# Converting the early weight tiles first and letting attention normalise later, in a fused attention and two-layer kernel

## The chip, the cores and the metric

The kernel runs on one core of one Trainium2 chip. The metric is the time of one execution in device microseconds; the time quoted for a kernel is the median of its runs. A profile is one execution with the hardware profiler on; its span is measured from the first to the last instruction shown.

## The reference

Batch 2, 8 heads, 768 positions, head size 64. Attention with a local window of 96 positions and 8 global ones, then two dense layers, all in float32:

```python
scores = q @ k.T / 8 - slope[h] * dist;  outside the window: -1e9
a = softmax(scores);  x = (a @ v) as 1536 tokens x 512
h = x @ w_in;   x = (h * tanh(softplus(h))) @ w_out      # layer 1, d_ff 2048
h = x @ w_in2;  out = softplus(h) @ w_out2               # layer 2
```

## The kernel before

**Attention** works in 24 steps. A step is one batch, one pair of heads and two query tiles of 128 rows, so four score tiles, each against at most 232 keys. `scores` (L462) puts them into PSUM, `soft` adds the bias and takes the row extreme on VectorE (L481) and the exponential with its row sum on ScalarE (L492). `norm` adds 1e-9 to the four sums on GpSimd (L501), takes the reciprocal on VectorE (L503) and multiplies the four tiles on GpSimd (L506). `transposes` turns the tiles on TensorE (L522) and copies them to SBUF on ScalarE or VectorE (L525), `values` multiplies by v (L539), and `store_x` writes x as a rounded half and a rest (L553 ScalarE, L554 VectorE). In one turn of the loop the program writes down the scores of step i, `norm` of step i-1, `transposes` of i-2, `values` of i-3 and `store_x` of i-4. The tiles of probabilities have LAG+2 = 4 buffers, the small tiles m and z three each (pool `sb`). The loads of q, k, v and the raw weights all go through one DMA queue, that of SP.

**The dense layers** see 3 blocks of 512 tokens. Each layer has 16 weight tiles f; tile f has two halves, part 0 for the up product (w_in) and part 1 for the down product (w_out). A chunk s is one layer, one block and one f. `up(s)` is 12 matmuls (L247) into one PSUM bank; `chunk(s)` is the activation and the split of its result into a rounded half and a rest (for layer 1: four VectorE instructions L104, L106, L109, L115, four ScalarE ones L102, L107, L110, L282, one GpSimd L283); `down(s)` is 12 matmuls (L267) into four banks `yp`. Program order puts `down(s-3)` behind `up(s)`.

**Weights** arrive as float64 bit patterns and are made into float32 pairs by the core itself, in 64 units of one half tile. A unit is three VectorE instructions (L145, L150, L154, 128x512 each), a ScalarE copy (L209) and a GpSimd subtraction (L211); `fill(upto)` advances this by ticks, four to a unit. The units of layer 1 are in the order (0,0) (1,0) (2,0) (3,0) (0,1) (4,0) (1,1) (5,0) (2,1) (6,0) (3,1) (7,0) (4,1) (8,0) (5,1) ..., written as (tile, part). Tiles 0 to 6 (EARLY = 7) have SBUF of their own; tiles 7 to 14 use the pool `wb`, which is opened only when attention has given its SBUF back.

**Beside each other.** `norm` carries `fill` with a goal that rises to 4*PRE = 40 ticks, so 10 units, by the end of attention; `early` writes the first AHEAD = 4 chunks into the attention loop, at turns 15, 17, 19 and 21. From chunk 4 on the goal rises by RATE1 = 8 ticks, so two units, with each chunk. This is program order. The framework makes the queue of each engine from it: an instruction with a higher place in program order is preferred, one that is ready earlier by its own model of the durations may go ahead of it, except that the first instruction of each unit keeps its place among its kind. Once the queues are made, each engine runs its queue in order.

Of the kernel before, what the change touches and what calls it, by code (L numbers as in the profile page):

```python
# [11 lines left out]
F32 = mybir.dt.float32  # L12
# [8 lines left out]
P = 128  # L21
# [4 lines left out]
NK = G + W + P  # L26
# [4 lines left out]
FC = DFF // P  # L31
TB = 512
# [3 lines left out]
WMIN2 = float((np.array([0x38100000], np.int32).view(np.float32) ** 2)[0])  # L36
CUTS = ((0, P + NK, 0, 2 * P), (P + NK, P + 3 * NK, 2 * P, 4 * P), (P + 3 * NK, KX, 4 * P, S))
SKEW = 3
PRE = 10
EARLY = 7  # L40
DLAG = 3
LAG = 2
AHEAD = 4
FROM = 15
HPO = 60
RATE1 = 8.0
RATE2 = 4.5
WEIGH = ((14, 1.2, 24), (65, 1.45, 40))

# [109 lines left out]
def fast_path(tc, small, qT, kx, vx, w1, w2, out, ng, nl, two, load_flag):  # L159
    nc = tc.nc  # L160
    far_side = bass.opposite_side(tc.default_side)
    with ExitStack() as outer:
# [8 lines left out]
        raw = {}  # L171

        units = []
        for n in range(0, 2 * FC, FC):
            for f in range(FC + SKEW):
                units += [(n + f, 0)] if f < FC else []
                units += [(n + f - SKEW, 1)] if f >= SKEW else []

        turns = []
        for i in range(2):  # L180
# [41 lines left out]
        def xy_tile(name):  # L222
            return xy.tile([P, CC, 2, TB], F32R, tag="xy", name=name)

        x = [xy_tile(f"x{i}") for i in range(NB)]
# [4 lines left out]
        gp = outer.enter_context(tc.tile_pool(name="gp", bufs=2))  # L230
# [4 lines left out]
        g = {}  # L235
# [103 lines left out]
        def early(i):  # L339
            s, odd = divmod(i - FROM, 2)  # L340
            if 0 <= s < AHEAD and not odd:
                up(s)
                chunk(s, 0)

        attention(tc, qT, kx, vx, ng, nl, x, fetch, fill, early)

        wpool.append(outer.enter_context(tc.tile_pool(name="wb", bufs=FC - EARLY - 1)))
        op = outer.enter_context(tc.tile_pool(name="op", bufs=1))
# [4 lines left out]
        for s in range(DLAG, NS + DLAG):  # L353
# [6 lines left out]
            if AHEAD <= s < NS:  # L360
                up(s)
                r = s - (NB - 1) * FC
                goal = 4 * PRE + int(RATE1 * (s + 1 - AHEAD))
                if goal > 8 * FC:
# [9 lines left out]
        return general  # L374


def attention(tc, qT, kx, vx, ng, nl, x, fetch, fill, early):
    nc = tc.nc
    with ExitStack() as st:
        cst = st.enter_context(tc.tile_pool(name="cst", bufs=1))  # L380
        kv = st.enter_context(tc.tile_pool(name="kv", bufs=2))
        sb = st.enter_context(tc.tile_pool(name="sb", bufs=3))
        pts = st.enter_context(tc.tile_pool(name="pts", bufs=4))
        ps = st.enter_context(tc.tile_pool(name="ps", bufs=LAG + 2))
        pss = st.enter_context(tc.tile_pool(name="pss", bufs=1, space=PSUM))
# [7 lines left out]
        def load_qk(bh):  # L393
            if bh >= B * HP:
                return
            b, hp = bh // HP, bh % HP
            ktile[bh] = kv.tile([P, KX], F32, tag="k", name=f"k{bh}")
            qtile[bh] = kv.tile([P, S], F32, tag="q", name=f"q{bh}")
            cuts = CUTS if bh == 0 else ((0, KX, 0, S),)
            for k0, k1, q0, q1 in cuts:  # L400
                nc.sync.dma_start(ktile[bh][:, k0:k1], kx[b, hp, :, k0:k1])
                nc.sync.dma_start(qtile[bh][:, q0:q1], qT[b, hp, :, q0:q1])

        def load_v(bh):
            if bh >= B * HP:
                return
            vtile[bh] = kv.tile([P, NV, P], F32, tag="v", name=f"v{bh}")
            nc.sync.dma_start(vtile[bh], vx[bh // HP, bh % HP])
# [5 lines left out]
        load_qk(1)  # L414
        load_v(1)

        ci = cst.tile([P, P], F32, name="ci")
        rel = cst.tile([P, NK + P], F32, name="rel")
        nc.gpsimd.iota(rel[:, :NK], [[-1, NK]], base=G + W, channel_multiplier=1, allow_small_or_imprecise_dtypes=True)
        nc.gpsimd.iota(rel[:, NK:], [[-1, P]], base=0, channel_multiplier=1, allow_small_or_imprecise_dtypes=True)  # L420
        nc.gpsimd.iota(ci, [[1, P]], base=0, channel_multiplier=0, allow_small_or_imprecise_dtypes=True)
        far = cst.tile([P, NK + P], F32, name="far")
        dist = cst.tile([P, NK + P], F32, name="dist")
        nc.vector.tensor_scalar(out=dist, in0=rel, scalar1=0.0, scalar2=1000.0, op0=ALU.is_lt, op1=ALU.mult)
        nc.vector.tensor_tensor(out=rel, in0=rel, in1=dist, op=ALU.add)
        nc.vector.memset(far[:, G:NK], BIG)
# [8 lines left out]
        def slope(h):  # L435
            engine = nc.vector if h < 2 else nc.gpsimd
            engine.tensor_scalar(
                out=d8[:, h, :], in0=dist, scalar1=-8.0 * 2.0 ** -(h + 1), scalar2=1.0, op0=ALU.mult, op1=ALU.mult
            )
# [6 lines left out]
        n = len(steps)  # L446
# [3 lines left out]
        def geom(t):  # L450
            return (P, P, 1) if t == 0 else (NK, CH, 2)

        def scores(i):
            b, hp, t0 = steps[i]
            bh = b * HP + hp
            for u in range(2):
                t = t0 + u
                w, _, _ = geom(t)
                off = 0 if t == 0 else P + (t - 1) * NK
                for j in range(2):  # L460
                    rows = slice(64 * j, 64 * j + 64)
                    nc.tensor.matmul(  # L462
                        sp[:, j, u, :w],
                        qtile[bh][rows, t * P : (t + 1) * P],
                        ktile[bh][rows, off : off + w],
                        start=True,
                        stop=True,
                    )

        def soft(i):  # L470
            b, hp, t0 = steps[i]
            p = ps.tile([P, 4, NK], F32, tag="p", name=f"p{i}")
            m = sb.tile([P, 4], F32, tag="m", name=f"m{i}")
            z = sb.tile([P, 4], F32, tag="z", name=f"z{i}")
            exps = []
            for u in range(2):
                w, _, _ = geom(t0 + u)
                off = NK if t0 + u == 0 else 0
                for j in range(2):
                    c = 2 * u + j  # L480
                    nc.vector.tensor_tensor_reduce(  # L481
                        out=p[:, c, :w],
                        in0=sp[:, j, u, :w],
                        in1=d8[:, 2 * hp + j, off : off + w],
                        scale=-0.125,
                        scalar=3.0e38,
                        op0=ALU.add,
                        op1=ALU.min,
                        accum_out=m[:, c : c + 1],
                    )  # L490
                    exps.append(
                        lambda c=c, w=w: nc.scalar.activation(  # L492
                            p[:, c, :w], p[:, c, :w], AF.Exp, bias=m[:, c : c + 1], scale=-1.0, accum_out=z[:, c : c + 1]
                        )
                    )
            prob[i], psums[i] = p, z
            return exps

        def norm(i, goal):
            p, z = prob[i], psums.pop(i)  # L500
            nc.gpsimd.tensor_scalar(out=z, in0=z, scalar1=1e-9, scalar2=1.0, op0=ALU.add, op1=ALU.mult)  # L501
            fill(goal)
            nc.vector.reciprocal(z, z)  # L503
            for c in range(4):
                w, _, _ = geom(steps[i][2] + c // 2)
                nc.gpsimd.tensor_scalar(  # L506
                    out=p[:, c, :w],
                    in0=p[:, c, :w],
                    scalar1=z[:, c : c + 1],
                    scalar2=1.0,  # L510
                    op0=ALU.mult,
                    op1=ALU.mult,
                )

        def transposes(i):
            p = prob.pop(i)
            for u in range(2):
                _, ch, nch = geom(steps[i][2] + u)
                tp = pst.tile([P, 4, P], F32, tag="t", name=f"t{i}_{u}")
                for j in range(2):  # L520
                    for c in range(nch):
                        nc.tensor.transpose(tp[:ch, j * nch + c, :], p[:, 2 * u + j, c * ch : (c + 1) * ch], ident)  # L522
                t = pts.tile([P, 4, P], F32, tag="pt", name=f"pt{i}_{u}")
                copy = nc.vector.tensor_copy if (2 * i + u) % 3 == 2 else nc.scalar.copy
                copy(t[:ch, : 2 * nch, :], tp[:ch, : 2 * nch, :])  # L525
                pt[i, u] = t
# [28 lines left out]

        for i in range(n + LAG + 3):
            exps = []
            if i < n:
                scores(i)
                exps = soft(i)  # L560
                if i % per == per - 1:
                    load_qk(i // per + 2)
                if i + 2 < H:
                    slope(i + 2)
            if 0 <= i - 1 < n:
                norm(i - 1, 4 * PRE * max(0, i - 2) // (n - 2))
            for e in exps[:2]:
                e()
            if 0 <= i - LAG < n:
                transposes(i - LAG)  # L570
            for e in exps[2:]:
                e()
            if 0 <= i - LAG - 1 < n:
                values(i - LAG - 1)
                if (i - LAG - 1) % per == per - 1:
                    load_v((i - LAG - 1) // per + 2)
            if 0 <= i - LAG - 2 < n:
                store_x(i - LAG - 2)
            early(i)
# [182 lines left out]
```

## Time and profile before

| | |
|---|---|
| median of 3 runs | 649.25 us (648.32, 649.25 and one of 1016.29) |
| profiled execution: time, span | 647.7 us, 645.9 us |
| TensorE matmul busy | 614.1 us, 95% |
| TensorE weight load busy | 488.3 us, 76% |
| VectorE busy | 481.5 us, 75% |
| ScalarE busy | 344.0 us, 53% |
| GpSimd busy | 267.0 us, 41% |

Busy time is the time in which the engine had an instruction running; on TensorE matmuls overlap, so its busy share says that it had work, not that it went at its full rate. PE is TensorE, PEld its weight loads, DVE VectorE, ACT ScalarE, POOL GpSimd, SP the queue that issues the DMAs. A number after L is a line of the kernel.

### The profile page before, as it was taken

Reading aid. Unit: us, or ns where it says so; the run is one execution under the profiler, and the core shown is the slowest. Engines: PE = TensorE matmul, PEld = TensorE weight load, DVE = VectorE, ACT = ScalarE, POOL = GpSimd, SP = SyncE. Lnnn points to the kernel's source line nnn. Section 1 sums busy time; section 2 is a strip of 40 time slices with the busy share of each in tenths; the row PEclk is TensorE's granted clock in tenths of the full one; section 3 lists DMA queues with packets and bytes.
Section 4 is the critical chain, followed back from the end, with each engine's and each line's share of the span. In section 5 each row is a group of like instructions: output and inputs, shape, how many; then the busy total and the mean of one; then the engine's idle time right before and its main releaser. Section 6 shows DMA issues by size and latency. Waiting matters only on the chain. (4 is left out here: it accounts for less than half of the span.)

```text
span 645.9 us, 9028 instructions
## 1 busy us (share of the span) xinstructions
PE 614.1 (95%) x3026; PEld 488.3 (76%) x3026; DVE 481.5 (75%) x998; ACT 344.0 (53%) x715; POOL 267.0 (41%) x297
## 2 busy tenths in 40 slices
PE   5999897969999999999999999999999999999994
PEld 3666675856678888888888888888888888888883
DVE  4788888089999775656897998988778865756642
ACT  4779886155545544444555665555554444444441
POOL 5566666146654232222553554654523222132221
PEclk9999799979999999999999999999999999999998
DMA  8747513035555353431342432432445544644301
GB/s 287 231 166 280 199 48 112 21 97 157 163 170 164 129 162 100 130 98 65 90 135 70 128 101 70 142 114 71 128 142 180 165 131 131 227 132 130 131 1 71
DMA packets 24390, 85.11 MB, mean 132 GB/s; under 512 B 2832, under 2 KB 3600, under 8 KB 24336
## 3 DMA queue, kind: packets, MB, share of 16 engines
q1 hardware_dynamic: 24336, 84.46, 40.7%
q8 instruction: 26, 0.43, 0.3%
q14 instruction: 28, 0.23, 0.1%
HBM read 81.30 MB, written 3.15 MB: 131 GB/s over the span
## 5 line engine op out<-in xcount | busy, mean ns | idle before, releaser
L283 POOL TENSOR_TENSOR g<-e,g 128x512 fp32r<-128x512 f32 x96 | 131.0, 1365 | 256.2 <-ACT g L282 250.5
L247 PE MATMUL h<-x,w 128*128 128x512 f32 x576 | 146.6, 399 | 3.5 <-POOL w L211 2.2
L267 PE MATMUL yp<-g,w 128*128 128x512 f32 x576 | 142.5, 397 | 6.5 <-ACT w L209 5.5
L267 PE MATMUL yp<-w,g 128*128 128x512 f32 x576 | 139.6, 390 | 1.3 <-POOLq L97 0.7
L247 PE MATMUL h<-y,w 128*128 128x512 f32 x576 | 139.2, 390 | 0.0
L267 PEld LDWEIGHTS yp<-g,w 128*128 128x128 f32 x576 | 108.8, 191 | 33.1 <-ACT w L209 6.7
L247 PEld LDWEIGHTS h<-x,w 128*128 128x128 f32 x576 | 108.2, 191 | 30.8 <-POOL w L211 4.6
L267 PEld LDWEIGHTS yp<-w,g 128*128 128x128 f32 x576 | 107.8, 188 | 25.1 <-POOLq L97 1.1
L247 PEld LDWEIGHTS h<-y,w 128*128 128x128 f32 x576 | 108.1, 188 | 22.8
L211 POOL TENSOR_TENSOR w<-a,w 128x512 fp32r<-128x512 f32 x64 | 84.6, 1322 | 74.4 <-ACT w L209 73.7
L282 ACT CAST g<-e 128x512 fp32r<-128x512 f32 x96 | 59.4, 618 | 48.6 <-PE yp L267 44.4
L209 ACT CAST w<-a 128x512 fp32r<-128x512 f32 x64 | 39.6, 619 | 42.5 <-DVE a L154 42.1
L127 DVE SCALAR_TENSOR_TENSOR h<-h,t 128x512 f32<-128x512 f32 x48 | 33.5, 697 | 35.5 <-ACT t L125 35.4
L107 ACT ACTIVATE t<-e,two 128x512 f32<-128x512 f32 x48 | 34.7, 725 | 43.2 <-DVE e L106 43.2
L119 ACT ACTIVATE e<-h 128x512 f32<-128x512 f32 x48 | 28.5, 594 | 43.8 <-PE h L247 33.6
L102 ACT ACTIVATE e<-h 128x512 f32<-128x512 f32 x48 | 28.4, 596 | 41.9 <-PE h L247 28.9
L492 ACT ACTIVATE p<-p,m 128x232 f32<-128x232 f32 (+1 forms) x96 | 44.5, 466 | 11.3 <-DVE m L481 11.1
L115 DVE TENSOR_TENSOR e<-h,t 128x512 f32<-128x512 f32 x48 | 33.0, 687 | 23.0 <-ACT t L110 22.4
L506 POOL TENSOR_SCALAR p<-p,z 128x232 f32<-128x232 f32 (+1 forms) x96 | 42.5, 461 | 15.8 <-DVE z L503 14.6
L125 ACT ACTIVATE t<-t 128x512 f32<-128x512 f32 x48 | 30.3, 631 | 34.9 <-DVE e L124 34.8
L315 DVE CUSTOM_DVE_ANT_0 top<-top 128x512 f32<-128x512 f32 x64 | 47.9, 767 | 0.0
L145 DVE TENSOR_SCALAR bits<-raw 128x512 int32<-128x512 int32 x64 | 44.0, 688 | 4.7 <-DMA raw<-w 4.3
(64 smaller groups left out, 633.8 us busy)
## 6 DMA issues: line engine op xcount, KB each, us to landing
raw<-w SPq DMA_DIRECT2D x64, 512.0 KB, 3.5
top<-w SPq DMA_DIRECT2D x64, 512.0 KB, 3.6
v<-vx SPq DMA_DIRECT2D x8, 704.0 KB, 5.9
k<-kx SPq DMA_DIRECT2D x7, 644.0 KB, 3.8
out<-o SPq DMA_DIRECT2D x12, 256.0 KB, 3.6
q<-qT SPq DMA_DIRECT2D x7, 384.0 KB, 4.4
k<-kx SPq DMA_DIRECT2D x2, 232.0 KB, 3.6
q<-qT SPq DMA_DIRECT2D x3, 128.0 KB, 3.7
```

Of the source, the lines that this page charges most:

```text
L107: nc.scalar.activation(t, e, AF.Ln, bias=two)
L127: nc.vector.scalar_tensor_tensor(out=h, in0=h, scalar=0.0, in1=t, op0=ALU.max, op1=ALU.add)
L145: nc.vector.tensor_scalar(out=t, in0=top, scalar1=3, scalar2=0x3FFFFFF8, op0=ALU.logical_shift_left, op1=ALU.bitwise_and)
L209: nc.scalar.copy(w[:, 0, half], a)
L211: nc.gpsimd.tensor_tensor(out=w[:, 1, half], in0=a, in1=w[:, 0, half].bitcast(F32), op=ALU.subtract)
L247: nc.tensor.matmul(h, w[:, a, c * P : (c + 1) * P], src[:, c, b, :], start=(n == 0), stop=(n == 3 * CC - 1))
L267: ins = nc.tensor.matmul(yp[s // FC][c], lhsT, rhs, start=(f == 0 and a + b == 0), stop=(f == FC - 1 and b == 1))
L282: nc.scalar.copy(gg[:, 0, :], e)
L283: nc.gpsimd.tensor_tensor(out=gg[:, 1, :], in0=e, in1=gg[:, 0, :].bitcast(F32), op=ALU.subtract)
L315: nc.vector.tensor_tensor_reduce(out=top, in0=top, in1=top, scale=-1.0, scalar=-3.0e38, op0=ALU.mult, op1=ALU.max, accum_out=lows[:, u : u ...
L492: lambda c=c, w=w: nc.scalar.activation(p[:, c, :w], p[:, c, :w], AF.Exp, bias=m[:, c : c + 1], scale=-1.0, accum_out=z[:, c : c + 1])
L506: nc.gpsimd.tensor_scalar(out=p[:, c, :w], in0=p[:, c, :w], scalar1=z[:, c : c + 1], scalar2=1.0, op0=ALU.mult, op1=ALU.mult,)
```

## The change

The units of tiles 0 to 6 come first, both parts, then those of tiles 7 to 15. The first 11 units are the same as before; then come (4,1) (5,1) (6,1) and only then (7,0) (8,0) (9,0) (10,0) (7,1) .... Attention's fill goal rises to 4*14 ticks over one turn more, and the goal after it by 7 ticks with each chunk. `norm` works two steps behind the scores, `transposes` three, `values` four, `store_x` five; the loop has one turn more, the tiles of probabilities have one buffer more, and the early chunks stand at turns 16, 18, 20 and 22. Four constant tiles of attention's set-up move into the two buffers of the pool `gp`, which the chunks' results use later.

```diff
-PRE = 10
+PRE = 14
 EARLY = 7
 DLAG = 3
-LAG = 2
+LAG = 3
 AHEAD = 4
-FROM = 15
+FROM = 16
 HPO = 60
-RATE1 = 8.0
+RATE1 = 7.0
...
-        for n in range(0, 2 * FC, FC):
-            for f in range(FC + SKEW):
-                units += [(n + f, 0)] if f < FC else []
-                units += [(n + f - SKEW, 1)] if f >= SKEW else []
+        for first, last in ((0, EARLY), (EARLY, FC), (FC, 2 * FC)):
+            for n in range(first, last + SKEW):
+                units += [(n, 0)] if n < last else []
+                units += [(n - SKEW, 1)] if n - SKEW >= first else []
...
-        attention(tc, qT, kx, vx, ng, nl, x, fetch, fill, early)
+        attention(tc, qT, kx, vx, ng, nl, x, fetch, fill, early, gp)
...
-        ci = cst.tile([P, P], F32, name="ci")
-        rel = cst.tile([P, NK + P], F32, name="rel")
+        spare = [gp.tile([P, 2 * TB], F32, tag="g", name=f"spare{i}") for i in range(2)]
+        rel, far, ci = spare[0][:, : NK + P], spare[0][:, TB : TB + NK + P], spare[1][:, TB : TB + P]
+        dist = spare[1][:, : NK + P]
...
-        far = cst.tile([P, NK + P], F32, name="far")
-        dist = cst.tile([P, NK + P], F32, name="dist")
...
-            if 0 <= i - 1 < n:
-                norm(i - 1, 4 * PRE * max(0, i - 2) // (n - 2))
+            if 0 <= i - 2 < n:
+                norm(i - 2, 4 * PRE * max(0, i - 2) // (n - 1))
```

## Rows read from the trace of the kernel before

**Rows 1.** Stretches: busy us (instructions) by engine, granted clock, DMA share, GB/s.

```profile
20.00:40.00 20.00, 18.42 (x153) 11.98 (x150) 15.78 (x69) 15.70 (x56) 11.90 (x27) 1.00 0.65 207
40.00:60.00 20.00, 20.00 (x187) 14.26 (x185) 16.40 (x64) 16.69 (x62) 14.91 (x32) 1.00 0.63 229
60.00:80.00 20.00, 16.98 (x111) 12.11 (x110) 16.64 (x58) 17.21 (x55) 12.32 (x22) 0.83 0.61 208
80.00:95.00 15.00, 15.00 (x122) 11.36 (x121) 11.88 (x42) 11.46 (x34) 10.68 (x21) 1.00 0.14 42
95.00:112.00 17.00, 14.04 (x128) 10.15 (x125) 15.39 (x43) 12.43 (x38) 11.00 (x19) 1.00 0.36 118
112.00:131.00 19.00, 18.38 (x91) 14.40 (x90) 4.29 (x9) 4.18 (x9) 2.58 (x2) 1.00 0.10 29
...
141.00:185.60 44.60, 41.49 (x169) 30.42 (x168) 41.31 (x68) 24.32 (x41) 26.82 (x21) 1.00 0.51 157
...
200.00:500.00 300.00, 299.92 (x1320) 247.43 (x1320) 238.73 (x394) 158.10 (x268) 120.39 (x89) 1.00 0.37 116
```

**Rows 2.** TensorE in order of time: start, us, what [idle before <-releaser].

```profile
112.92 4.90 PE L267 MATMUL yp<-g,w 128*128 128x512 f32 x20 [0.51 <-ACT x L553]
117.75 1.09 PE L539 MATMUL xhalf<-pt,v 116*64 116x128 f32 x16
118.78 6.45 PE L267 MATMUL yp<-g,w 128*128 128x512 f32 x27
125.06 2.88 PE L247 MATMUL h<-x,w 128*128 128x512 f32 x12
...
128.01 2.88 PE L247 MATMUL h<-x,w 128*128 128x512 f32 x12
135.99 5.16 PE L267 MATMUL yp<-g,w 128*128 128x512 f32 x12 [5.10 <-ACT w L209]
140.98 2.92 PE L247 MATMUL h<-x,w 128*128 128x512 f32 x12
```

**Rows 3.** The stretch of that wait in slices of 5 us, columns as in rows 1.

```profile
135.00:140.00 5.00, 4.01 (x10) 3.10 (x11) 4.93 (x9) 2.70 (x5) 2.10 (x2) 0.50 0.41 123
```

**Rows 4.** VectorE in order of time, columns as in rows 2.

```profile
110.45 0.69 DVE L154 SCALAR_TENSOR_TENSOR a<-raw,bits 128x512 int32<-128x512 int32 x1
...
128.61 0.92 DVE L104 TENSOR_SCALAR t<-e 128x512 f32<-128x512 f32 x2 [7.72 <-ACT e L102]
...
132.67 0.68 DVE L145 TENSOR_SCALAR bits<-raw 128x512 int32<-128x512 int32 x1
```

**Rows 5.** VectorE until 112.8 us, by line: count, busy us, mean ns, idle before.

```profile
L145 DVE TENSOR_SCALAR bits<-raw 128x512 int32<-128x512 int32 x12 | 8.3, 691 | 0.4 <-DMA raw<-w 0.4
L150 DVE SCALAR_TENSOR_TENSOR bits<-raw,bits 128x512 int32<-128x512 int32 x12 | 8.3, 690 | 0.1
L154 DVE SCALAR_TENSOR_TENSOR a<-raw,bits 128x512 int32<-128x512 int32 x12 | 8.2, 683 | 0.2
...
L503 DVE RECIPROCAL z<-z 128x4 f32<-128x4 f32 x24 | 4.1, 173 | 12.0 <-POOL z L501 11.6
...
L106 DVE SCALAR_TENSOR_TENSOR e<-e,t 128x512 f32<-128x512 f32 x5 | 3.5, 696 | 0.1
L109 DVE TENSOR_TENSOR h<-e,h 128x512 f32<-128x512 f32 x5 | 3.4, 688 | 0.1
L115 DVE TENSOR_TENSOR e<-h,t 128x512 f32<-128x512 f32 x5 | 3.4, 684 | 0.1
L104 DVE TENSOR_SCALAR t<-e 128x512 f32<-128x512 f32 x5 | 2.2, 447 | 0.5 <-ACT e L102 0.4
```

**Rows 6.** GpSimd and ScalarE late in attention, in order of time.

```profile
98.36 1.58 POOL L506 TENSOR_SCALAR p<-p,z 128x128 f32<-128x128 f32 x4 [0.38 <-DVE z L503]
99.90 1.27 POOL L211 TENSOR_TENSOR w<-a,w 128x512 fp32r<-128x512 f32 x1
...
101.98 0.49 ACT L492 ACTIVATE p<-p,m 128x232 f32<-128x232 f32 x1 [0.35 <-DVE m L481]
```

More of the change, by code (lines that the diff above doesn't have):

```diff
@@ L374, in fast_path, with attention @@
         return general
-def attention(tc, qT, kx, vx, ng, nl, x, fetch, fill, early):
+def attention(tc, qT, kx, vx, ng, nl, x, fetch, fill, early, gp):
     nc = tc.nc
```

## Prediction

> **What bounds the kernel now.** I read the stretches first [rows 1]. From 200 to 500 us TensorE is never idle: 1320 matmuls in 300 us, 227.3 ns each, all of 512 columns. The change touches nothing there, so this is the pace against which the rest is measured. The loss lies ahead of it, in three places.
>
> The first is attention. Between 20 and 112 us VectorE is busy for 15.78 + 16.40 + 16.64 + 11.88 + 15.39 = 76.1 of 92 us and TensorE for 84.4 of 92 [rows 1]. Neither is full throughout; from 60 to 80 us the mean granted clock is 0.83.
>
> The second is the hand-over. The order of TensorE's work [rows 2] shows 48 matmuls of down 0 to 3 (20, 27, and one that lies between the two ups of 12 each behind them), the two ups, and then 5.10 us of nothing, ended by the ScalarE copy of a weight half (L209). It is (4,1), the thirteenth unit: down(4) needs it. The twelve matmuls that follow take 5.16 us until the next group begins about 5.0 us later, and the granted clock of that slice is 0.50, so 1.2 of 2.4 GHz [rows 3]. From 112.92 to 140.98 TensorE did 48 + 24 + 12 = 84 matmuls, worth 84 x 0.2273 = 19.1 us, and 1.09 us of attention: 28.06 - 20.2 = **7.9 us lost**.
>
> Why was (4,1) late? VectorE ended the last instruction of the twelfth unit, (7,0), at 111.1, and began (4,1) at 132.67 [rows 4]. In between it stood 7.72 us before L104, for the exponential of a chunk whose up came at 125.06 behind the downs [rows 2, 4]; in the stretch from 112 to 131 us it worked 4.29 of 19 us [rows 1]. The unit had no missing input that the trace names; it stood behind the chunk in VectorE's queue.
>
> The third is the stretch from 141 to 185.6 us. TensorE does 168 matmuls (169 by the window's count, one at its edge), worth 38.2 us, in 44.6: **6.4 us lost**. VectorE is busy 41.31 of 44.6 [rows 1], so it is the bound. Per chunk it has 0.447 + 0.696 + 0.688 + 0.684 = 2.52 us, and two units of 0.691 + 0.690 + 0.683 = 2.06 us [rows 5], 6.64 us together, where TensorE needs 24 x 0.2273 = 5.46. The measured period is 44.6 / 7 = 6.37 us (VectorE's instructions overlap slightly).
>
> **The change part by part.**
>
> *The order of units.* The first eleven are as before. Twelfth to fourteenth become (4,1), (5,1), (6,1), whose SBUF is there from the start, in place of (7,0), (4,1), (8,0). By 112.8 us the kernel before had already converted 12 units on VectorE, two more than its goal of 10 [rows 5]. With the new goal of 14, the halves for down(4), down(5) and down(6) are there when attention ends, and the wait of rows 2 has no cause: behind the two ups TensorE has down(4) to down(6), 36 x 0.2273 = 8.2 us of work, as cover for (7,0) and those behind it. With the wait goes the half-rate group. Gain between 0 (another late thing takes its place, say the result of chunk 5, which needs VectorE as well) and 7.9 us. I take 7, nearest to the full end, since the two late things in the rows are this half tile and the clock that followed.
>
> *RATE1 from 8 to 7.* Units per chunk fall from 2 to 1.75, VectorE's demand from 6.64 to 2.52 + 3.61 = 6.13 us, still over 5.46. Scaled from the measured period that is 6.37 x 6.13 / 6.64 = 5.88, a gain of 0.49 us for each of seven chunks, **3.4 us**. Bounds: 0 if VectorE again begins late and has the same backlog, 6.4 if it begins at 112 us and TensorE never sees it. The units left after attention are 18 against 20 not yet converted there in the kernel before.
>
> *More units inside attention.* Between 12 (what is there now) and 14 lie 2 x 2.06 = 4.1 us of VectorE; if the queue again runs two ahead of its goal, 16, 8.2 us. Each also has 1.27 us on GpSimd [rows 6] and a ScalarE copy. VectorE has 15.9 us free between 20 and 112 [rows 1], so some of it is hidden; where VectorE is full, it is not.
>
> *The deeper lag.* Nothing is added but a turn of the loop: the same instructions, each further from its producer. What it can remove is waiting on the chain from exponential to transpose: VectorE stood 11.6 us before its 24 reciprocals for GpSimd's sums [rows 5]. That is the cover for the extra units. I count 4.1 us of units less a part of these waits, 2.6 us, **+1.5 us** for attention as a whole. Bounds: +8.2 (four units on the path, no wait saved) and -6.4 (about two thirds of the 11.6 us returned beyond the units' cost, in turns where VectorE is what ends last). One edge gets tighter: z has three buffers still, and the exponential of step i can write only when GpSimd's multiplies of step i-3 are done. They now stand one turn later.
>
> *SP's queue.* The raw loads of the extra units (512 KB each) go into the one DMA queue ahead of later q, k and v loads. Its share in attention is 0.65 at most over 20 us and 0.14 to 0.36 in the later part [rows 1]; I cost them at nothing. If that cover is gone, a late k or v stops a step, as any late load would.
>
> *FROM and the constants in `gp`.* Four constant tiles take the two buffers that chunks 2 and 3 use later; the last reader is GpSimd's bias of head 7 in turn 5. Nothing, unless a chunk wanted them before.
>
> **Sum.** -7.0 - 3.4 + 1.5 = -8.9 us on a span of 645.9, which goes to 637.0; the profiled execution's 647.7 to 638.8. The median of the runs is 1.55 us above that execution, so the forecast is 649.25 - 8.9 = **640 us**.
>
> **The rivals.**
>
> *Attention tightens as well.* With more slack TensorE waits for less, and VectorE starts on units in the hand-over. The whole loss of 7.9 + 6.4 goes and attention shrinks by about 4 us: 649.25 - 18.3 = 631. For it: 11.6 us of reciprocal waits, and 14.7 us of idle VectorE in the hand-over [rows 1, 5]. Against: from 95 to 112 us VectorE is already busy 15.39 of 17 [rows 1]. In weight loads TensorE is far from full in attention: 59.9 of 92 us, 65%, where the dense stretch has 247.4 of 300, 82% [rows 1]; at the dense share the same loads would fit in 59.9 / 0.825 = 72.6 us, so up to 19 us are there. The Trainium skill (Perfetto Trace Analysis, Identifying the Most-Contended Engine) says to judge TensorE's headroom by weight-load occupancy and not by matmul busy time. By that rule attention has the room that this rival needs; by busy time (84.4 of 92) it has 7.6 us. The trace does not decide, since attention's matmuls are of other shapes.
>
> *The gap moves.* PE's downs again stand ahead of the up that feeds VectorE, chunk 5's result is late instead of a weight half, and attention pays for its units: -3.4 + 4.1, so 650 us. For it: the 7.72 us before L104 come from the order of TensorE's queue, which the diff does not fix [rows 2, 4]. That the order of units does not do what it says is this case too.
>
> *Slower: the sums' buffers.* GpSimd's multiplies of step 21 ended at 99.94 and the exponential of step 23 began at 101.98, 2.0 us later [rows 6]; with the new lag those multiplies stand where step 20's are needed by step 23, so this is the margin. If a unit's GpSimd subtraction of 1.27 us and a late sum use it up, ScalarE stands before the exponential, and the copies behind it in its queue with it. A subtraction each for 14 units is 17.8 us on the chain; with the units' 8.2 us and 7.9 us of the hand-over won, 649.25 + 18.1 = 667. It decides from the point where those multiplies end more than 2.0 us later than now relative to the scores. GpSimd is busy 60.8 of 92 us in attention [rows 1], which speaks against it in most steps.
>
> **How the numbers follow.** Forecast (634 to 646) 0.53, attention tightens (625 to 634) 0.21, the gap moves (646 to 656) 0.19, slower (656 to 675) 0.07. Two per cent, about what a measurement of this kernel can tell from no change, is 13 us: faster means below 636.3, slower above 662.2. Faster is the second case, 0.21, and the lower end of the first, 0.05: 0.26. Slower is most of the last, 0.05. The rest is 0.69. The range that leaves out about 0.1 on each side runs from 630 to 653.
>
> **What would show it.** After attention no TensorE wait of over 2 us on a copy of L209; down(4) to down(6) run without one; the clock stays at full rate around it. By the last instruction of attention at least 14 runs of L154, in place of 12. Attention's last matmul between 110 and 120 us in place of 118.8. A period of about 5.9 us per chunk in the VectorE-bound stretch. The reciprocal's wait well under 11.6 us. Wrong would be: attention longer by over 8 us, ScalarE waiting before L492 for GpSimd's L506, or a new idle stretch of TensorE in front of an up that waits for (7,0) or (8,0).

## The result and the profile after

| | before | after |
|---|---|---|
| median | 649.07 us (4 runs) | 641.63 us (4 runs) |
| profiled execution: time, span | 647.7, 645.9 us | 642.0, 640.1 us |

The changed kernel takes 0.9887 of the time of before (95% interval 0.9868 to 0.9906): a gain of 1.1%, less than the 2% that the prediction took as its limit, but clear of no change. The forecast was 640 us in a range of 630 to 653. One early run of the kernel before took 1016 us; it is left out of the ratio, and without it the median before is 648.89 us, so the medians differ by 7.3 us.

The stretches of the changed kernel, columns as in rows 1:

```profile
20.00:40.00 20.00, 18.25 (x152) 11.95 (x151) 17.23 (x69) 16.32 (x56) 13.34 (x29) 1.00 0.69 217
40.00:60.00 20.00, 18.45 (x166) 12.94 (x163) 18.05 (x70) 16.70 (x61) 15.95 (x34) 1.00 0.73 259
60.00:80.00 20.00, 18.94 (x157) 13.65 (x157) 19.21 (x69) 19.29 (x66) 14.03 (x26) 1.00 0.59 208
80.00:95.00 15.00, 14.73 (x114) 11.27 (x113) 14.76 (x44) 13.42 (x38) 13.42 (x24) 1.00 0.35 108
95.00:112.00 17.00, 12.49 (x99) 9.26 (x98) 12.21 (x31) 9.54 (x29) 8.50 (x14) 0.80 0.31 103
112.00:131.00 19.00, 19.00 (x105) 15.13 (x106) 4.01 (x8) 2.78 (x6) 3.84 (x3) 1.00 0.20 58
...
141.00:185.60 44.60, 41.44 (x174) 31.55 (x174) 42.20 (x68) 25.17 (x42) 24.94 (x20) 1.00 0.50 149
...
200.00:500.00 300.00, 299.81 (x1320) 247.38 (x1319) 237.89 (x394) 158.16 (x268) 120.02 (x88) 1.00 0.37 115
```

Against [rows 1] VectorE is busier in attention (17.23 + 18.05 + 19.21 + 14.76 + 12.21 = 81.5 of 92 us, where it was 76.1), the dense stretch is the same, and between 112 and 131 us VectorE is as idle as before: 4.01 of 19 us, against 4.29.

TensorE behind attention, columns as in rows 2:

```profile
111.88 5.36 PE L267 MATMUL yp<-g,w 128*128 128x512 f32 x22 [0.88 <-DVE pt L524]
117.17 1.09 PE L538 MATMUL xhalf<-pt,v 116*64 116x128 f32 x16
118.19 5.50 PE L267 MATMUL yp<-g,w 128*128 128x512 f32 x23
123.62 1.09 PE L538 MATMUL xhalf<-pt,v 116*64 116x128 f32 x16
124.64 3.69 PE L267 MATMUL yp<-g,w 128*128 128x512 f32 x15
128.17 5.60 PE L247 MATMUL h<-x,w 128*128 128x512 f32 x24
136.36 3.04 PE L247 MATMUL h<-x,w 128*128 128x512 f32 x12 [2.59 <-DVE e L115]
139.24 4.92 PE L267 MATMUL yp<-g,w 128*128 128x512 f32 x21
...
161.67 2.56 PE L247 MATMUL h<-x,w 128*128 128x512 f32 x10 [0.35 <-POOL w L211]
...
168.06 2.60 PE L247 MATMUL h<-x,w 128*128 128x512 f32 x10 [0.61 <-POOL w L211]
...
174.48 2.56 PE L247 MATMUL h<-x,w 128*128 128x512 f32 x10 [0.63 <-POOL w L211]
```

The 5.10 us wait for a weight half and the half-rate group behind it [rows 2, 3] are gone: down 0 to 4, 60 matmuls, run before the first late up, and none waits on L209. What is left there is 2.59 us before an up that has no free bank of PSUM (the memory TensorE writes its products to) until VectorE has ended a chunk (L115). From 161.67 to 174.48 the ups follow each other every 6.4 us, and each waits for GpSimd's half of a weight (L211).

VectorE there, in order of time:

```profile
114.29 0.69 DVE L154 SCALAR_TENSOR_TENSOR a<-raw,bits 128x512 int32<-128x512 int32 x1
118.71 0.42 DVE L553 TENSOR_TENSOR x<-xhalf,x 128x256 fp32r<-128x256 f32 x1 [3.74 <-ACT x L552]
125.17 0.42 DVE L553 TENSOR_TENSOR x<-xhalf,x 128x256 fp32r<-128x256 f32 x1 [6.03 <-ACT x L552]
126.57 0.42 DVE L553 TENSOR_TENSOR x<-xhalf,x 128x256 fp32r<-128x256 f32 x1 [0.98 <-ACT x L552]
132.18 0.92 DVE L104 TENSOR_SCALAR t<-e 128x512 f32<-128x512 f32 x2 [5.18 <-ACT e L102]
```

It stands from 115.0 to 132.2 us but for three short stores: for the last steps' x, whose `values` lie between the downs in TensorE's queue, and then for the exponential of a chunk whose up came at 128.17. VectorE until 112.8 us, by line, as in rows 5:

```profile
L154 DVE SCALAR_TENSOR_TENSOR a<-raw,bits 128x512 int32<-128x512 int32 x15 | 10.2, 680 | 0.2
...
L502 DVE RECIPROCAL z<-z 128x4 f32<-128x4 f32 x24 | 4.2, 173 | 8.2 <-POOL z L500 7.8
```

15 units are through, where there were 12 (a sixteenth ends at 115.0), and the reciprocals' wait fell from 11.6 to 7.8 us [rows 5].

### The profile page after: what moved, and what is told of

It is laid out like the page before. It is cut to its first block, busy times and chain, and to the rows that moved or that the text cites. A ratio compares the mean times of both kernels' runs of the same rounds, so it can differ in the third digit from the quotient of the medians.

```text
span 640.1 us, 9030 instructions
## 1 busy us (share of the span) xinstructions
PE 609.8 (95%) x3026; PEld 487.4 (76%) x3026; DVE 481.3 (75%) x998; ACT 343.8 (54%) x715; POOL 267.1 (42%) x297
## 5 line engine op out<-in xcount | busy, mean ns | idle before, releaser
L247 PE MATMUL h<-x,w 128*128 128x512 f32 x576 | 142.9, 394 | 6.0 <-DVE e L115 2.9
L267 PE MATMUL yp<-w,g 128*128 128x512 f32 x576 | 139.6, 390 | 1.5 <-POOLq L97 0.7
L267 PE MATMUL yp<-g,w 128*128 128x512 f32 x576 | 139.2, 391 | 1.7 <-DVE pt L524 0.9
L247 PEld LDWEIGHTS h<-x,w 128*128 128x128 f32 x576 | 106.6, 188 | 32.1 <-POOL w L211 4.1
L267 PEld LDWEIGHTS yp<-g,w 128*128 128x128 f32 x576 | 107.6, 188 | 26.1 <-POOL w L211 1.3
L267 PEld LDWEIGHTS yp<-w,g 128*128 128x128 f32 x576 | 107.8, 188 | 25.2 <-POOLq L97 1.1
L211 POOL TENSOR_TENSOR w<-a,w 128x512 fp32r<-128x512 f32 x64 | 84.9, 1328 | 68.8 <-ACT w L209 67.4
L282 ACT CAST g<-e 128x512 fp32r<-128x512 f32 x96 | 59.4, 620 | 47.3 <-PE yp L267 41.5
L209 ACT CAST w<-a 128x512 fp32r<-128x512 f32 x64 | 39.6, 620 | 38.5 <-DVE a L154 38.3
L119 ACT ACTIVATE e<-h 128x512 f32<-128x512 f32 x48 | 28.6, 596 | 43.8 <-PE h L247 33.6
L115 DVE TENSOR_TENSOR e<-h,t 128x512 f32<-128x512 f32 x48 | 33.0, 687 | 22.9 <-ACT t L110 22.4
L102 ACT ACTIVATE e<-h 128x512 f32<-128x512 f32 x48 | 28.5, 597 | 38.8 <-PE h L247 26.6
```

What stands on the lines that cost most here:

```text
L209: nc.scalar.copy(w[:, 0, half], a)
L211: nc.gpsimd.tensor_tensor(out=w[:, 1, half], in0=a, in1=w[:, 0, half].bitcast(F32), op=ALU.subtract)
L247: nc.tensor.matmul(h, w[:, a, c * P : (c + 1) * P], src[:, c, b, :], start=(n == 0), stop=(n == 3 * CC - 1))
L267: ins = nc.tensor.matmul(yp[s // FC][c], lhsT, rhs, start=(f == 0 and a + b == 0), stop=(f == FC - 1 and b == 1))
L282: nc.scalar.copy(gg[:, 0, :], e)
```

## The experiments

To compare kernels whose TensorE queues differ, each span is divided into three parts. **A**, attention: the start of the first down, plus 1.09 us for each step of `values` that comes later, less 0.2273 us for each matmul of an up that came earlier. The dense work: 96 chunks of 24 matmuls, 2304 in all, at the pace of [rows 1], 523.7 us, the same for all. **L**, what is left: the time lost from the hand-over on. Some 10 us of L, before and after, lie behind the stretches that are looked at here, at the block changes and the end of the kernel. Before: A = 112.92 + 1.09 - 72 x 0.2273 = 97.6, L = 645.9 - 97.6 - 523.7 = 24.6. These are of one profiled execution each. Three kernels have the same instructions in the same order on every engine (the change, the run with 8 ticks and the one with four buffers for the sums); they differ by up to 1.0 us in A and 1.6 in L, so less than that means nothing.

| kernel | first down | ups before | values later | span | A | L | median us | ratio (95%) |
|---|---|---|---|---|---|---|---|---|
| before | 112.92 | 72 | 1 | 645.9 | 97.6 | 24.6 | 649.07 | 1 |
| the change | 111.88 | 72 | 2 | 640.1 | 97.7 | 18.7 | 641.63 | 0.9887 (0.9868 to 0.9906) |
| order and goal, old lags | 115.32 | 72 | 0 | 637.2 | 99.0 | 14.5 | 639.82 | 0.9876 (0.9860 to 0.9893) |
| lags alone | 108.95 | 72 | 2 | 644.7 | 94.8 | 26.2 | 646.62 | 0.9977 (0.9965 to 0.9989) |
| change, 8 ticks | 110.87 | 72 | 2 | 638.6 | 96.7 | 18.2 | 641.61 | 0.9907 (0.9881 to 0.9933) |
| change, other bank | 110.10 | 84 | 2 | 632.6 | 93.2 | 15.7 | 635.03 | 0.9802 (0.9780 to 0.9824) |
| order and goal, bank | 121.71 | 84 | 0 | 640.4 | 102.6 | 14.1 | 640.50 | 0.9869 (0.9852 to 0.9885) |
| bank alone | 113.30 | 84 | 1 | 638.9 | 95.3 | 19.9 | 640.42 | 0.9865 (0.9848 to 0.9881) |
| change, four sums | 111.19 | 72 | 2 | 640.5 | 97.0 | 19.8 | 641.51 | 0.9883 (0.9862 to 0.9903) |
| change, goal 10 | 111.87 | 72 | 2 | 658.1 | 97.7 | 36.7 | 658.58 | 1.0138 (1.0116 to 1.0160) |
| lags and bank | 111.58 | 84 | 2 | 640.9 | 94.7 | 22.5 | 643.45 | 0.9919 (0.9903 to 0.9936) |
| change, bank, goal 12 | 113.36 | 84 | 2 | 635.3 | 96.5 | 15.1 | 637.56 | 0.9840 (0.9814 to 0.9866) |
| change, bank, goal 13 | 113.09 | 84 | 2 | 638.0 | 96.2 | 18.1 | 640.69 | 0.9880 (0.9863 to 0.9897) |
| order alone, goal 10 | 113.49 | 72 | 1 | 655.5 | 98.2 | 33.6 | 657.47 | 1.0131 (1.0104 to 1.0157) |

**Order and goal without the lags.**

```diff
-LAG = 3
+LAG = 2
-FROM = 16
+FROM = 15
-            if 0 <= i - 2 < n:
-                norm(i - 2, 4 * PRE * max(0, i - 2) // (n - 1))
+            if 0 <= i - 1 < n:
+                norm(i - 1, 4 * PRE * max(0, i - 2) // (n - 2))
```

> The changed kernel with the lags of before (normalise one step behind, transpose two, early chunks at turns 15 to 21, goal in attention over 22 turns); the order of units, the goal of 14 units and the constants' place are those of the change. Theory A (the gain is the hand-over's: the halves for down 4 to 6 are ready): 641 to 645 us, no TensorE wait on the copy of L209 behind the first ups. Rival B (the gain needs the lag, since the extra units hold up attention without it): 647 to 652 us, attention's last transposes 4 us or more later.

Measured 639.82 us, ratio 0.9876, 1.2 us below the range of theory A. Its interval and that of the change overlap over most of their length: the lags add nothing that can be seen to the order with the goal. A is 1.3 us over before, hardly more than the noise, L 10.1 under. The hand-over of this kernel, TensorE in order of time:

```profile
115.32 8.35 PE L267 MATMUL yp<-g,w 128*128 128x512 f32 x29
123.50 2.88 PE L247 MATMUL h<-x,w 128*128 128x512 f32 x12
126.22 4.47 PE L267 MATMUL yp<-g,w 128*128 128x512 f32 x19
130.53 2.88 PE L247 MATMUL h<-x,w 128*128 128x512 f32 x12
```

There is no wait at all in it, as theory A had said, though VectorE stands 9.09 us before L104 in this kernel too, until 127.05 us: 16 units were through, and TensorE had work. Rival B is out.

**The lags alone.** The units' loop, the goal of 10 and the 8 ticks are put back:

```diff
-PRE = 14
+PRE = 10
-RATE1 = 7.0
+RATE1 = 8.0
-        for first, last in ((0, EARLY), (EARLY, FC), (FC, 2 * FC)):
...
+        for n in range(0, 2 * FC, FC):
...
```

> The changed kernel with the old order of units, the goal of 10 units in attention and 8 ticks per chunk; only the lags, the turns of the early chunks and the constants' place are changed. Theory A: the wait of down(4) for its weight half is there as before, 647 to 651 us. Rival B (the lag is what gained): 641 to 644 us, with attention's end 3 us or more earlier than in the kernel before.

646.62 us, 0.9977, between the two forecasts and 0.4 us from theory A's. A falls by 2.8 us, so the deeper lag does shorten attention. But the old wait is there, and longer:

```profile
133.81 5.49 PE L267 MATMUL yp<-g,w 128*128 128x512 f32 x12 [5.75 <-ACT w L209]
```

L is 1.6 us higher, no more than kernels with the same queues differ by; the span is 1.2 us shorter. VectorE stands behind attention here as well: its last unit, the twelfth, begins its last instruction at 109.70 us, and the next L104 comes at 126.46.

**Eight ticks per chunk.**

```diff
-RATE1 = 7.0
+RATE1 = 8.0
```

> The changed kernel with 8 ticks per chunk in place of 7. Theory A of the prediction (the goal sets VectorE's load, 6.13 against 6.64 us per chunk): 644 to 646 us. Rival C (a chunk uses up two units whatever the goal says, one for its up and one for its down, and VectorE's queue has them in the same order): within 1 us of the changed kernel, 641 to 643 us, with the same period of 6.4 us per chunk.

641.61 us against 641.63. Rival C holds; theory A's term is nothing. The ups of this kernel:

```profile
160.71 2.56 PE L247 MATMUL h<-x,w 128*128 128x512 f32 x10 [0.35 <-POOL w L211]
...
167.10 2.60 PE L247 MATMUL h<-x,w 128*128 128x512 f32 x10 [0.61 <-POOL w L211]
...
173.53 2.58 PE L247 MATMUL h<-x,w 128*128 128x512 f32 x10 [0.60 <-POOL w L211]
```

The period is 6.4 us with 7 ticks, with 8 ticks and in the kernel before [rows 1], and in the traces every engine has the same instructions in the same order for 7 and 8: the edit changes nothing that runs, and this run is a repeat of the change. The goal is not what sets the rate. With 7 ticks it is 56 + 7 x 7 = 105 ticks at chunk 10, 26 units; VectorE began the last instruction of its eleventh chunk (L115) at 157.03 us with 21 units through (L154). It is behind the goal, and a lower goal takes nothing from it. A chunk needs one half for its up and one for its down; when there is no stock of halves, it costs two units: from that L115 to the one at 182.14 us there are four chunks and eight units.

**Another bank for chunk 5.**

```diff
-        h = hps[s >= AHEAD and s % 3 == 2].tile([P, TB], F32, tag="h", name=f"h{s}")
+        h = hps[s > AHEAD and s % 3 == 1].tile([P, TB], F32, tag="h", name=f"h{s}")
```

Of three banks for h the third is free only when attention's last x is stored. In both kernels of the case up(5) is the first that needs it; here it is up(7).

> The changed kernel with another choice of the PSUM bank for h: chunks 5 and 6 use the two banks that are there during attention, and the bank freed by attention's last step serves chunks 7, 10, 13 and so on. Theory D (VectorE is idle in the hand-over because up(5) has to wait for attention's last bank, and the 2.59 us wait of TensorE comes from that): 636 to 640 us, that wait gone and VectorE's idle stretch after 114 us shorter by 4 us or more. Rival E (VectorE stands in front of the last stores of x anyway, so the bank changes nothing): 641 to 643 us.

635.03 us, ratio 0.9802: the fastest of all, clear of the change by its interval, and 1 us below theory D's range. Rival E is out. TensorE in it:

```profile
97.94 3.03 PE L247 MATMUL h<-x,w 128*128 128x512 f32 x12
...
126.39 0.62 PE L247 MATMUL h<-x,w 128*128 128x512 f32 x2
126.84 1.98 PE L267 MATMUL yp<-g,w 128*128 128x512 f32 x8
128.65 5.15 PE L247 MATMUL h<-x,w 128*128 128x512 f32 x22
...
163.13 0.73 PE L247 MATMUL h<-x,w 128*128 128x512 f32 x2 [0.86 <-ACT w L209]
```

and the end of VectorE's stand:

```profile
122.55 0.43 DVE L104 TENSOR_SCALAR t<-e 128x512 f32<-128x512 f32 x1 [5.20 <-ACT e L102]
```

One up more (84 matmuls, not 72) runs inside attention, at 97.94, where the changed kernel was about to stand: its TensorE waited 2.23 and 1.00 us between 98 and 103 us, and its granted clock in the two slices of 5 us from 100 to 110 us was 0.65 and 0.67. With the other bank it is 1.00 in both. The changed kernel's slices, columns as in rows 1:

```profile
100.00:105.00 5.00, 3.18 (x24) 2.62 (x25) 2.42 (x6) 2.70 (x10) 3.23 (x7) 0.65 0.36 102
105.00:110.00 5.00, 4.61 (x32) 3.38 (x30) 3.89 (x7) 1.94 (x5) 0.19 (x1) 0.67 0.02 7
```

VectorE goes on at 122.55 instead of 132.18, and TensorE has no wait of any size until 163. A is 4.5 us lower than in the change, L 3.0.

The 5.20 us that are left are not this bank's. The exponential that VectorE waits for (L102, at 121.92) is of a chunk whose up ran at 97.94. ScalarE stood before it at the copy of an earlier chunk's result (L282, at 119.90), 3.01 us for a down (L267), and then 1.39 us for GpSimd. The results have two buffers from chunk 2 on (pool `gp`), and chunk 4's can be written when down(2) is done. More buffers there were not tried.

**The bank alone, in the kernel before, and with the old lags.** The same line as above, in the kernel before and in the first experiment's.

> The kernel before with only the other choice of the PSUM bank for h. Theory D (the chunk that VectorE waited for kept (4,1) behind it): with chunk 5 early, (4,1) is converted before down(4) needs it even in the old order, 640 to 645 us. Rival A (the order of units alone decides): the wait on L209 stays and it is 647 to 650 us.

> The new order of units and goal of 14 with the lags of before, and the other choice of the PSUM bank for h (chunks 5 and 6 on the banks that are there during attention). Theory D (the late up(5) keeps VectorE idle whatever the lag): 633 to 637 us, VectorE's wait of 9.1 us before L104 behind attention's end gone or halved. Rival F (without the lag TensorE has no gap after attention, so nothing is left to gain): 639 to 641 us.

Alone it takes the kernel before to 640.42 us, 0.9865, as theory D had it: one line does as much as the whole change, with the order of units and the goal of before. VectorE has converted (4,1) and one unit more by 120.4 us, ahead of the chunk that it waits for until 125.72:

```profile
119.76 0.68 DVE L154 SCALAR_TENSOR_TENSOR a<-raw,bits 128x512 int32<-128x512 int32 x1
...
125.72 0.43 DVE L104 TENSOR_SCALAR t<-e 128x512 f32<-128x512 f32 x1 [4.95 <-ACT e L102]
```

and down(4), the twelve matmuls at 128.31, has no wait and does not run at half rate:

```profile
117.44 8.31 PE L267 MATMUL yp<-g,w 128*128 128x512 f32 x35
125.59 2.88 PE L247 MATMUL h<-x,w 128*128 128x512 f32 x12
128.31 2.88 PE L267 MATMUL yp<-g,w 128*128 128x512 f32 x12
```

With order and goal but the old lags it gives 640.50, 0.9869, nothing beyond the order: rival F's figure, and theory D's time missed, though VectorE's wait of 9.1 us is gone as it had said. A and L show why: L is 14.1 (TensorE never waits from 121.71 to 193 us), no less than the 14.5 without the bank's line within the noise, as rival F had it, and A is 102.6: an up of 12 matmuls stands at 101.89, and among the transposes and values behind it TensorE waits 1.44 us for GpSimd and 2.37 us for a store of x. Why the framework's order came out so was not followed further.

**Lags and bank.**

> The old order of units with goal 10 and 8 ticks per chunk, the lags of the change, and the other choice of the PSUM bank for h: the last of the eight combinations of order, lag and bank. Theory D+ (the lag shortens attention by about 3 us and the bank takes the hand-over's gap, so both count): 636 to 639 us. Rival H (either the order or the bank takes the gap, and the lag is lost behind it, as in the run with the lag alone): 640 to 642 us.

643.45 us, 0.9919, worse than either rival's figure and than the bank alone; A is 94.7, but L is 22.5. A wait for a weight half is back: 2.22 us on L209 at 141.90, and the twelve matmuls behind it take 4.88 us. So of the eight combinations of order with goal, lags and bank, all three together are the best (0.9802); every other change lies between 0.9865 and 0.9977. The lags are worth 0.7% behind both others, 0.2% alone, nothing behind the order, and cost 0.5% behind the bank.

**Four buffers for the sums.**

```diff
-        sb = st.enter_context(tc.tile_pool(name="sb", bufs=3))
+        sb = st.enter_context(tc.tile_pool(name="sb", bufs=4))
```

> The changed kernel with four buffers in place of three for the small tiles of extremes and sums; the queues of all engines have the same order. The slower rival of the prediction (the exponential waits for GpSimd's multiplies three steps back): 640 us or less, by 0.5 us or more for each step where it happened. Theory A (that edge is never the last): 641 to 643 us, no difference.

641.51 us, no difference. In the changed kernel ScalarE's exponentials wait for VectorE's extremes alone. The slower rival of the prediction did not occur.

**A goal of 10, with and without the lags.** The change with the old goal, and the new order alone, which has the lags, FROM and `norm`'s line of before as well:

```diff
-PRE = 14
+PRE = 10
-RATE1 = 7.0
+RATE1 = 8.0
```

> The changed kernel with the goal in attention back at 10 units and 8 ticks per chunk; order and lags are those of the change. Theory A (it is the order that makes (4,1) to (6,1) ready, and the higher goal that puts them into attention): the halves come late again, a wait of TensorE on L209 or L211 of 2 us or more behind attention, 644 to 649 us. Rival G (VectorE's free time at the end of attention does them in any case): 640 to 643 us, with attention's end up to 3 us earlier.

> The new order of units and the constants' place, everything else as in the kernel before (lags, goal of 10 units, 8 ticks per chunk): the order by itself. Theory K (VectorE takes about 12 units by the end of attention whatever their order, stands still behind it, and the place of the thirteenth unit then decides; the order pays only with the goal of 14): 650 to 660 us, with TensorE waits of over 4 us on the copy of L209. Theory A as the prediction put it (the order makes the halves of down 4 to 6 ready by itself): 640 to 646 us.

658.58 and 657.47 us, ratios 1.0138 and 1.0131: **the order by itself makes the kernel slower**, by 1.4% with the lags and 1.3% without. The first is beyond both of its forecasts (theory A's sign, a late half, came true, its size not); the second is as theory K had it. TensorE in the second one:

```profile
136.54 8.32 PE L267 MATMUL yp<-g,w 128*128 128x512 f32 x24 [5.12 <-ACT w L209]
144.70 5.60 PE L247 MATMUL h<-x,w 128*128 128x512 f32 x24
156.46 1.22 PE L247 MATMUL h<-x,w 128*128 128x512 f32 x2 [6.16 <-ACT w L209]
158.51 7.15 PE L247 MATMUL h<-x,w 128*128 128x512 f32 x22 [0.83 <-POOL w L211]
```

Both kernels had 12 units through VectorE when attention ended, as the kernel before and the one with the lags alone had. The thirteenth, (5,1), came behind the idle stretch, so down(5) waited, 5.12 us; and now the halves for the ups are the last in the row, so an up waits too, 6.16 us. With the lags these waits are 8.02 and 6.17 us. In the old order no wait of over 0.6 us follows the one of 5.10 until 200 us. Between the waits the clock was low for a part: 24 matmuls took 8.32 us, with a granted clock of 0.52 from 135 to 140 us, and the next 24 took 5.60.

**Fewer units with the other bank.** Goals of 12 and 13 in place of 14, with the bank's line:

> The changed kernel with the other bank and a goal of 12 units in attention in place of 14. Theory I (with up(5) early the extra units are not needed in attention and only lengthen it, 2.06 us of VectorE each): 632 to 634 us. Rival J (as with the goal of 10, units that come after attention come late): 637 us or more, a TensorE wait on L209 or L211 of 2 us or more.

> The changed kernel with the other bank and a goal of 13 units. Theory I: 633 to 635 us; rival J: 635 to 637 us.

637.56 and 640.69 us. Neither theory: there is no wait of over 2 us (rival J), but attention is 3 us longer with fewer units, not shorter (theory I). With 12 units L is the same as with 14 within the noise. So what a goal does to attention is not the sum of the units' durations. That it acts through the order that the framework makes is likely but was not followed; for 12, 13 and 14 the time does not run one way. Why 13 is the worst was not found.

## Why the prediction was right, and where it was not

**What bounds the kernel**: right. The dense stretch did not move, and the 5.8 us by which the span fell lie in the hand-over and the stretch behind it: L went from 24.6 to 18.7, A from 97.6 to 97.7.

**The order of units, -7.0**: the mechanism was right, the size was off. In the kernel before TensorE lost 7.9 us from its first down to 140.98 us, where the VectorE-bound stretch begins. In the changed kernel, from 111.88 to 150.12, where it begins there, it did 144 matmuls (32.7 us) and 2.18 us of `values` in 38.24: 3.3 us lost, so 4.6 won. The rest is what the rival "the gap moves" foresaw in part, a wait for a chunk's result in place of a weight half, 2.59 us and at full clock; the prediction named that as the reason for a gain of 0 and then counted almost nothing for it. It booked the gain under the order, with the goal of 14 in its text. The runs show that the order is worth nothing without that goal: with the goal of 10 it had 12 units through and lost 1.3%. The goal of 14 without the order was not run. In the old order the twelfth unit is (7,0), whose SBUF is not there until attention has ended, so the order is what lets the goal rise.

**RATE1, -3.4**: wrong. The period did not change, 6.4 us, and 8 ticks in place of 7 cost nothing (641.61). The step that failed is "units per chunk fall from 2 to 1.75": VectorE is behind the goal there, and use sets the rate, two halves to a chunk. What the stretch gave, about 1 us (150.12 to 179.93: 108 matmuls in 29.81 us, 5.3 lost where 6.4 were), goes with a shorter stretch, 108 matmuls for 168; three more units were through when attention ended.

**Attention, +1.5**: +0.1. Taken alone, the lags take 2.8 us off A and the units (order and goal, old lags) add 1.3; the prediction had 2.6 and 4.1. The two do not add up to +0.1, and the units' part is hardly over the noise. The reciprocals' waits fell by 3.8 us, but this does not show that the lag took them away, as the prediction had it: they are 8.8 us with the lags alone, and 6.4, less than in the change, with order and goal and the old lags.

**The terms put at nothing.** SP's queue: from 20 to 112 us no engine waits more than 0.5 us for a DMA in the changed kernel, 0.4 before. FROM and the constants in `gp` were not run by themselves.

**The rivals.** Attention did not tighten in the change. It did with the lags alone (A of 94.8), with the bank alone (95.3), and most with the bank on top of the change: 93.2, where the rival's 4 us would make 93.6. Weight loads in attention fill 59.1 of 92 us in the changed kernel, 64%, as before. The room that the Trainium skill's rule (Perfetto Trace Analysis, Identifying the Most-Contended Engine) would see there stayed unused, and the trace still does not say whether it exists: the fastest kernel, too, kept attention's A within 5 us of the old one. The gap moved, with 2.59 us in place of 5.10. The sums' buffers were never last.

**What would show it.** Right: no wait on L209 over 2 us, at least 14 units, the reciprocals' wait, and a granted clock of 1.00 behind attention, in all slices from 110 to 170 us. Wrong: the period, and attention's last matmul, at 124.7 instead of 110 to 120; two steps' `values` instead of one lie behind downs in TensorE's queue. The low clock did not vanish but moved to 100 to 110 us, inside attention.

So that the total was right to 2 us is in part luck. The order gave 2.4 us less than its term and RATE1's stretch 2.3 less; attention cost 1.4 less, which made up for some of it: -8.9 forecast, -5.7 between the two profiled executions. The medians moved by 7.3, and the 1.6 us between these belong to no term. And what the wait goes back to, VectorE standing for a chunk whose up is late for want of attention's last PSUM bank, was seen in the prediction as a row but not taken as a lever.

## What to carry to other kernels

When an engine stands behind an instruction that waits, ask what the producer is waiting for, down to the buffer, before work is moved around the wait: here one PSUM bank gave alone what the moved work gave (1.35% against 1.1%), and with it nearly twice as much (2.0%). An order of preparations pays only as far as the goal behind it is met; what comes next after the last finished one decides. And before a goal is lowered to ease an engine, see whether the engine keeps up with it: here VectorE was behind it, and 7 and 8 ticks gave the same queues.

## What the hardware showed

VectorE's L106, which reads two operands from SBUF, took 0.68 us at some times and 1.2 us at others. In the changed kernel:

```profile
140.46 1.19 DVE L106 SCALAR_TENSOR_TENSOR e<-e,t 128x512 f32<-128x512 f32 x1
...
143.11 0.68 DVE L106 SCALAR_TENSOR_TENSOR e<-e,t 128x512 f32<-128x512 f32 x1
```

and GpSimd beside it:

```profile
139.63 1.47 POOL L211 TENSOR_TENSOR w<-a,w 128x512 fp32r<-128x512 f32 x1
143.66 1.31 POOL L211 TENSOR_TENSOR w<-a,w 128x512 fp32r<-128x512 f32 x1 [2.56 <-ACT w L209]
```

The long one lies from 140.46 to 141.65 across a GpSimd subtraction that ends at 141.10 and is itself longer than usual, 1.47 us; the short one is nearly over when the next subtraction begins. The Trainium skill (GPSIMD Engine Reference, Specifications) names contention between GpSimd and VectorE instructions with two SBUF inputs; these rows agree, at some 0.5 us for VectorE. So do L109 and L115, which read one of their two operands from PSUM: in the same execution none of their 48 each took over 0.70 us, though 32 of the 48 L115 ran beside a GpSimd subtraction; L106 took up to 1.63. No run here took one of the two away to show it.
